# A mixer kernel: the z1 phase in an order fixed at build time, with edits to the first weights, the out operands and the last product

## The chip, the cores and the metric

The kernel runs on one core of one Trainium2 chip. The metric is device microseconds of one execution; lower is better. The five runs before the change took 671.44, 673.53, 670.41, 671.85 and 672.18 us, median 671.85. The engines are named as the profile names them: PE multiplies matrices (PEld is its loading of weights), DVE works on vectors, ACT evaluates functions and copies, POOL is a third engine that is hardly used, and SP (SyncE) only issues DMAs.

## What is computed

Two branches read the same x of 2048 tokens by 1024 features, and a gate mixes them:

```
g   = sigmoid(sum(x * gate_w))                 # per token
qkv = x @ wqkv                                 # 32 heads of 32
a   = softmax(q . k of 8 tokens at distance 0, 2, .., 14) v  @ wo
z   = gelu(x @ w_in)                           # 3584 columns: z1 | z2
z2  = layernorm(z2)
b   = (z1 * (w_sp @ z2 + b_sp)) @ w_out        # w_sp mixes tokens, 2048 x 2048
out = g * a + (1 - g) * b
```

All inputs are bfloat16.

## The kernel before

**Stages.** In the profiled execution PE passes through these, in us from the start of the span: start-up to 15.3 (filler matmuls L313, transposes of x L221, first value tiles L298); query, key and value tiles (L288, L298), with the attention bands (L350) between them; value products from 86.7 to 117.4; further attention work to 195; the z2 half of x @ w_in to 277.4; the z1 half to 361.5; the spatial product w_sp @ z2 from 363 to 532; the output product, which takes w_out and wo together, to 666.6.

**Quads.** From 86.7 us on, matmuls come in "quads": a 2 by 2 block product done with seven products instead of eight, as Strassen and Winograd do. `strassen` (L434) and `chain` (L485) are generators that yield after each product, and `run` interleaves two of them. A product is a row of matmuls (L431) of 128 by 128 by 320, 448 or 512 columns that add up in one bank of PSUM. Four banks make a side, X, Y, Z and V, and two sides alternate. Sums of operand blocks are made ahead by DVE (`sums4`, L563 to L570); sums of results are formed by copying one bank into another (ACT, L449, L460, L470, L504), by DVE adding a saved share (L492; in z1 the share is saved by L1052), and by letting later products add on top. So a PE product waits for the ACT copy or the DVE addition that frees or seeds its bank.

**Start-up.** gw_s (the gate weights) and the first half of the first value weights wvp are issued on ACT's queue; SP issues the first rows of x, the second half of wvp, and more of x in a fixed chain. `keep_warm` (L311) issues filler matmuls into bank 7. The program then transposes x's first rows (`xpose(0)`), and the gate column is transposed and copied by L321 into wvp, which every value tile (`vp_tile`, L293) reads. `vp_tile(i)` puts the next `xpose` in its middle, after two of its eight matmuls. Query and key tiles (`qk_tile`, L284) take banks in turn from `half_bank`; L301 reads the bank of the value tiles.

**Order of the work.** Attention and quads are emitted while a planner is live: it keeps a clock for PE, ACT, DVE, SP and the DMA engines, each operation has a cost and a due time, `advance` (L750) emits what is due, and the order of each engine is pinned to that of emission (`settle`). `due` holds DMAs, `streams` the three attention streams (L690 to L703 are their DVE work), and `fill` single DVE operations that go in when they are ready. `drain` (L772) empties all of these. Before the change the planner is live up to the end of the first z1 block. There `drain` and `settle` are called, `live` is cleared, and everything behind is ordered by the scheduler, with a few dependencies and priorities put in by hand.

**z1.** Seven blocks `fp`, each two interleaved chain quads (token halves c = 0, 1), 14 products of four 512-column matmuls. Block fp needs its 128 columns of both halves of w1 (`load_w1`, two DMAs of 256 KB into one of three slots), their DVE sums (`w1_sums`), and at its end gelu (ACT, L1056) and a store of z1 (`z_d`) from one of two slots, one for each c. Meanwhile the layernorm of z2 is finished: 26 squares on ACT (L851), run in groups of five or six at the start of blocks 0 to 4 by `between`; moments on DVE and POOL, and 16 normalisations (L989), by `normalize` in fours. The raw w_sp is transposed by DMA (`load_raw`, L191, eight of them in this phase), and its four sums (`wsp_sums`, L1028, L1029, L1034, L1035) are 4096 columns each.

**Spatial and out.** Fourteen strassen quads, seven with c = 0 and then seven with c = 1, of 7 products of 8 matmuls. While c = 1 runs, SP loads the out weights in four pieces after quads 0 to 3, `out_sums` (L1185) forms ot3, a first sum and ot2 after quad 3, and `load_act(0)` fetches the first operand of the out phase after quad 5. ot2 and ot3, and slot 0 of those operands, stand in the place of z2h (the normalised z2), whose columns belong to the blocks fp in turn. The out phase is 8 strassen quads, each product 11 matmuls. The last product of the last quad ends in `c21`: ACT copies one half of the bank (L1257), DVE the other (L1258), and each is stored by its own queue.

Of the kernel before, what the change touches and what calls it, by code (L numbers as in the profile page):

```python
# [13 lines left out]
P = 128  # L14
S = 2048
# [43 lines left out]
def kernel(  # L59
# [109 lines left out]
    nc.scalar.dma_start(wvp[:, 0:4, 0:VP], wq_v[:, 0:4, 2 * D:2 * D + VP])  # L169
    first_dma(xn[:, 0:1, :], x_v[:, 0:1, :])  # L170
    first_dma(wvp[:, 4:8, 0:VP], wq_v[:, 4:8, 2 * D:2 * D + VP])
# [106 lines left out]
    half_bank = [0]  # L278
# [14 lines left out]
    def vp_tile(i, bank=None, middle=None):  # L293
        ps = bank() if bank else banks[i % 2]
        for kt in range(KT):
            if kt == KT // 4 and middle is not None:
                middle()
            nc.tensor.matmul(ps[:, 0:VP + 1], xT[:, kt, i * P:(i + 1) * P], wvp[:, kt, :], start=(kt == 0), stop=(kt == KT - 1))  # L298
# [17 lines left out]
    keep_warm(8)  # L316
    xpose(0)
    keep_warm(2)
    gwT = banks[1][:, 0:KT // 2].bitcast(BF)
    nc.tensor.transpose(gwT, gw_s[:], ident[0:KT, 0:KT])  # L320
    nc.vector.tensor_copy(wvp[:, :, VP:VP + 1], gwT.rearrange("p (k o) -> p k o", o=1))  # L321
    for i in range(4):
# [102 lines left out]
    last_w1 = [None]  # L425
# [8 lines left out]
    def strassen(A11, A12, A22, S1, S2, S3, S4, B11, B21, B22, T1, T2, T3, T4, vs, c11, c12, c21, c22, share=nc.scalar.copy, N=512, flip=False, turn=True, side=None):  # L434
# [35 lines left out]
        seed = nc.scalar.copy(V[:, n], Y[:, n])  # L470
# [8 lines left out]
        pe(dur)  # L479
        product(V, pairs(A22, T4), False, N)  # L480
# [291 lines left out]
    def drain():  # L772
        t = clock["PE"]
        while any(s[1] != () for s in streams) or fill or due:
# [46 lines left out]
    w1_slots = [reg(R_OFF + o, 2048).rearrange("p (k f c) -> p k f c", k=KT, f=2) for o in (36864, 30720, 32768)]  # L821

    def load_w1(fp):
        for f in range(2):
            last_w1[0] = sync.dma_start(w1_slots[fp % 3][:, :, f, :], win_v[:, :, HF * f + fp * P:HF * f + (fp + 1) * P])
# [3 lines left out]
    def w1_steps(fp):  # L829
        w, s = w1_slots[fp % 3], ws_slots[fp % 2]  # L830
        return sums4_steps([s[:, q] for q in range(4)], w[:, 0:4, 0], w[:, 4:8, 0], w[:, 0:4, 1], w[:, 4:8, 1])
# [145 lines left out]
    def normalize(n):  # L977
        sl = slice(n, n + 4)
        s1v = s1[:, 4 * n:4 * (n + 4)].rearrange("p (i c) -> p i c", c=4)
        first = nc.vector.tensor_reduce(mean[:, sl], s1v, AX.X, ALU.add)  # L980
        tc.add_manual_dep(first.ins, last_add[0].ins.name, NOSYNC, reason="behind the additions of the quads")
# [5 lines left out]
        for m in range(n, n + 4):  # L987
            ii = z2_row(m)
            nc.vector.tensor_scalar(z2h[:, ii, :], z2[:, ii, :], mean[:, m:m + 1], rstd[:, m:m + 1],  # L989
                                    ALU.subtract, ALU.mult)  # L990
# [25 lines left out]
    def load_raw(c, a):  # L1016
        row = 4 * c + (a % 4) + 8 * (a // 4)
        inst = sync.dma_start_transpose(raw_slots[c][:, :, a, :], wsp_v[row])
        for x in (last_store, last_w1):
# [300 lines left out]
```

## Time and profile before

| | |
|---|---|
| median of five runs | 671.85 us (670.41 to 673.53) |
| the profiled execution | 671.63 us, span 669.9 us |
| PE busy | 659.6 us, 98% |
| DVE / ACT busy | 448.8 / 293.5 us |
| z1 phase on PE | 277.4 to 361.5 us |
| matmuls of L431 | 2436, 498.9 us |

The span runs from the first to the last recorded instruction. Times in a view count from its start. A view of waits names the instruction that waited, and the one that released it. A window gives how long each engine was busy in a stretch of time, so a stretch in which PE is busy for all of its length has nothing to gain from order. Durations are of single instructions; matmuls overlap their neighbours, so the distance between starts, not the mean duration, is what a matmul costs PE.

### The profile page before, as it was taken

What the parts mean: (1) busy time and instruction counts of PE and PEld (TensorE: products, weight loads), DVE (VectorE), ACT (ScalarE), POOL (GpSimd) and SP (SyncE); (2) the same over time, 40 slices, a digit from 0 to 9 for tenths busy, and PEclk for the clock granted to TensorE, in tenths of its full rate; (3) what the DMA queues carried; (4) which work ended last, traced back from release to release, by engine and by line L of the source; (5) the groups of instructions that cost most, each with busy time, mean ns of one, the idle gap of its engine ahead of it and who ended that gap; (6) DMA issues with size and microseconds to landing.
All of it is one profiled execution on the core that took longest, in us unless ns stands there. A gap on an engine that the chain in (4) does not pass through costs nothing.

```text
span 669.9 us, 10729 instructions
## 1 busy us (share of the span) xinstructions
PE 659.6 (98%) x4185; PEld 316.4 (47%) x4185; DVE 448.8 (67%) x663; ACT 293.5 (44%) x620; POOL 6.8 (1%) x15
## 2 busy tenths in 40 slices
PE   8999999998999999999999999999999999999998
PEld 4544467443445555444444444444444444444443
DVE  2520799966999999996679676897766685333301
ACT  3454676555678677887854212121122112222221
POOL 1000000000000000001000000000000000000000
PEclk9999999998999999999999999999999999999999
DMA  9988563698487040449984478567346598943100
GB/s 236 163 215 224 111 152 96 159 240 180 90 219 181 9 141 14 95 123 243 239 212 158 99 167 167 134 184 223 89 136 162 95 198 194 207 107 100 37 32 31
DMA packets 235683, 98.15 MB, mean 147 GB/s; under 512 B 189792, under 2 KB 221936, under 8 KB 235632
## 3 DMA queue, kind: packets, MB, share of 16 engines
q1 hardware_dynamic: 234944, 97.01, 60.6%
q8 instruction: 32, 0.52, 0.3%
q10 hardware_dynamic: 688, 0.46, 0.2%
q14 instruction: 19, 0.16, 0.1%
HBM read 45.10 MB, written 36.61 MB: 122 GB/s over the span
## 4 chain that ended last, share of the span: by engine, by line
PE 94%; DVE 2%; DMA 2%; ACT 1%; issue 0%; SPq 0%; ACTq 0%
PE psum_all L431 72%; PE psum_all L288 16%; PE psum_all L298 3%; PE psum_all L350 1%; DMA band_d<-arena 1%; PE psum_all L313 1%; DVE arena L694 1%; ACT arena L358 1%; DMA arena<-o_d 0%; DVE psum_all L492 0%; PE psum_all L808 0%; ACT arena L300 0%; DVE arena L1136 0%; ACT L801 0%; DVE arena L1131 0%
## 5 line engine op out<-in xcount | busy, mean ns | idle before, releaser
L431 PE MATMUL psum_all<-arena 128*128 128x512 f16 (+5 forms) x2436 | 498.9, 367 | 1.6 <-DVE psum_all L492 1.0
L431 PEld LDWEIGHTS <-arena 128*128 128x128 f16 (+1 forms) x2436 | 238.2, 98 | 261.1 <-issue 4.2
L288 PE MATMUL psum_all<-arena 128*128 128x512 bf16 x512 | 116.1, 383 | 0.7 <-ACT gl_s L301 0.6
L288 PEld LDWEIGHTS <-arena 128*128 128x128 bf16 x512 | 48.8, 98 | 58.1 <-issue 3.0
L694 DVE TENSOR_TENSOR arena<-arena,att_A 128x2048 f16<-128x2048 bf16 (+1 forms) x44 | 73.4, 1704 | 0.3
L291 ACT CAST arena<-psum_all 128x512 bf16<-128x512 f32 x64 | 37.2, 585 | 49.7 <-PE psum_all L288 49.6
L567 DVE TENSOR_TENSOR arena<-arena 128x1024 f16<-128x1024 f16 (+3 forms) x36 | 20.6, 583 | 53.2 <-PE psum_all L431 32.2
L449 ACT COPY psum_all<-psum_all 128x512 f32<-128x512 f32 (+1 forms) x30 | 15.8, 527 | 78.4 <-PE psum_all L431 77.7
L801 ACT ACTIVATE arena<-psum_all 128x448 bf16<-128x448 f32 x64 | 34.2, 544 | 17.6 <-DVE psum_all L492 8.6
L1056 ACT ACTIVATE arena<-psum_all 128x512 bf16<-128x512 f32 x56 | 30.3, 599 | 21.7 <-DVE psum_all L492 10.8
L569 DVE TENSOR_TENSOR arena<-arena 128x1024 f16<-128x1024 f16 (+3 forms) x36 | 20.5, 581 | 28.0 <-PE psum_all L431 13.0
L492 DVE TENSOR_TENSOR psum_all<-psum_all,arena 128x448 f32<-128x448 f32 (+1 forms) x58 | 36.6, 659 | 3.7 <-PE psum_all L431 3.0
L358 ACT CAST arena<-psum_all 128x1988 f16<-128x1988 f32 (+3 forms) x25 | 33.9, 1356 | 7.8 <-DMA band_d<-arena 6.5
L698 DVE TENSOR_TENSOR arena<-arena 128x2048 f16<-128x2048 f16 (+1 forms) x22 | 37.2, 1704 | 0.1
L470 ACT COPY psum_all<-psum_all 128x512 f32<-128x512 f32 (+1 forms) x30 | 15.9, 529 | 46.1 <-PE psum_all L431 45.1
L460 ACT COPY psum_all<-psum_all 128x512 f32<-128x512 f32 (+1 forms) x30 | 15.8, 528 | 40.6 <-PE psum_all L431 40.0
L455 ACT COPY arena<-psum_all 128x512 f32<-128x512 f32 (+1 forms) x30 | 16.2, 543 | 35.4 <-PE psum_all L431 30.4
L851 ACT ACTIVATE arena<-arena 128x896 bf16<-128x896 bf16 x32 | 30.1, 951 | 0.0
L568 DVE TENSOR_TENSOR arena<-arena 128x1024 f16<-128x1024 f16 (+3 forms) x36 | 20.6, 582 | 8.1 <-PE psum_all L431 7.9
L1243 DVE TENSOR_TENSOR arena<-psum_all,arena 128x512 bf16<-128x512 f32 x8 | 5.5, 691 | 29.0 <-ACT psum_all L470 29.0
L298 PE MATMUL psum_all<-arena 128*128 128x385 bf16 x128 | 22.6, 327 | 0.3 <-DVE arena L321 0.3
L570 DVE TENSOR_TENSOR arena<-arena 128x1024 f16<-128x1024 f16 (+3 forms) x36 | 20.4, 579 | 1.7 <-PE psum_all L431 1.6
(88 smaller groups left out, 391.4 us busy)
## 6 DMA issues: line engine op xcount, KB each, us to landing
arena<-v_d SPq DMA_DIRECT2D x8, 960.0 KB, 6.7
z_d<-arena SPq DMA_DIRECT2D x14, 512.0 KB, 4.4
arena<-z_d SPq DMA_DIRECT2D x14, 512.0 KB, 4.3
zg_d<-arena SPq DMA_DIRECT2D x56, 128.0 KB, 2.2
arena<-zg_d SPq DMA_DIRECT2D x32, 224.0 KB, 3.2
band_d<-arena SPq DMA_DIRECT2D x28, 248.5 KB, 5.1
arena<-in_A_wqkv_dram SPq DMA_DIRECT2D x16, 256.0 KB, 4.2
o_d<-arena SPq DMA_DIRECT2D x4, 1024.0 KB, 6.3
```

Of the source, the lines that this page charges most:

```text
L288: nc.tensor.matmul(ps[:], w[:, t, kt, :], xT[:, kt, 512 * c:512 * (c + 1)], start=(kt == 0), stop=(kt == KT - 1))
L291: nc.scalar.copy(dst[:, :, 256 * c:256 * (c + 1)], ps[:].rearrange("p (n e) -> p e n", e=2))
L298: nc.tensor.matmul(ps[:, 0:VP + 1], xT[:, kt, i * P:(i + 1) * P], wvp[:, kt, :], start=(kt == 0), stop=(kt == KT - 1))
L358: nc.scalar.copy(dst, src)
L431: nc.tensor.matmul(bank[:, 0:N], lhsT, rhs, start=(start and m == 0), stop=(m == n - 1), skip_group_check=True)
L492: last_add[0] = nc.vector.tensor_tensor(out[:, n], a[:, n], vs, ALU.add)
L567: first = nc.vector.tensor_tensor(s_out[0], a21, a22, ALU.add)
L694: lambda ws=ws, in0=in0, in1=in1: tt(p5[:, ws], in0[:, ws], in1[:, ws], ALU.mult)), False
L698: lambda a=p3[:, ws], b=p3[:, ws.start + 4:ws.stop + 4]: tt(a, a, b, ALU.add)), not n
L801: nc.scalar.activation(z2[:, i + 8 * a, ZC * c:ZC * (c + 1)], bank[:, 0:ZC], ACT.Gelu_apprx_tanh, accum_out=s1[:, 4 * n + c:4 * n + c + 1])
L851: return nc.scalar.activation(junk, src, ACT.Square, accum_out=(s2, s2h)[x][:, n:n + 1])
L1056: last_gelu[0] = nc.scalar.activation(z1s[:, f, a, :], bank[:], ACT.Gelu_apprx_tanh)
```

## The change

- **First weights.** wvp comes in four pieces of two rows of blocks, the first on ACT's queue, the other three on SP's between x's first two loads. Six filler matmuls, the gate column and two more fillers precede the transposes of x. The first value tile does six of its eight matmuls before the next transposes. The query and key tiles begin one bank further on.
- **z1 phase.** The planner stays live through all seven blocks. After every second product one square is emitted (`z1_step`); moments and normalisations are put into `fill` when their squares are done, one normalisation at a time; the sums of w1 go to the head of `fill`, and the sums of w_sp for c = 0 become eight operations of 2048 columns in blocks 5 and 6. `drain` is called after block 1 and no longer empties `fill`.
- **w1.** Block 0 has its own slot. From there on, each half of w1 is loaded 256 columns wide, for blocks 1 and 2, 3 and 4, 5 and 6, in two DMAs of 512 KB.
- **Other transfers of that phase.** The eight transposes of w_sp are at fixed products of blocks 2 to 4, the z1 store slots are doubled, and the rows bsp and og are loaded after block 4.
- **Out operands.** ot2, ot3 and operand slot 0 move to z2h columns of blocks 0 to 4. ot2 and ot3 become four chunks of 128 columns, apart in memory (`spread`). All out weights are loaded after quads 0 and 1 of c = 1, the sums are made in three parts after quads 2, 3 and 4, and `load_act(0)` comes after quad 4.
- **Last product.** It is computed as two halves of 256 columns in two banks (`cut`), the upper half first. ACT copies the upper half, DVE the lower, and both are stored by SP.

Cut to what matters:

```diff
-    nc.scalar.dma_start(wvp[:, 0:4, 0:VP], wq_v[:, 0:4, 2 * D:2 * D + VP])
+    def load_wvp(k, dma):
+        dma(wvp[:, k:k + 2, 0:VP], wq_v[:, k:k + 2, 2 * D:2 * D + VP])
+    load_wvp(0, nc.scalar.dma_start)
     first_dma(xn[:, 0:1, :], x_v[:, 0:1, :])
-    first_dma(wvp[:, 4:8, 0:VP], wq_v[:, 4:8, 2 * D:2 * D + VP])
+    for k in range(2, KT, 2):
+        load_wvp(k, first_dma)
...
-    half_bank = [0]
+    half_bank = [1]
...
-            if kt == KT // 4 and middle is not None:
+            if kt == (2 if i else 6) and middle is not None:
...
-    keep_warm(8)
-    xpose(0)
-    keep_warm(2)
+    keep_warm(6)
     gwT = banks[1][:, 0:KT // 2].bitcast(BF)
     nc.tensor.transpose(gwT, gw_s[:], ident[0:KT, 0:KT])
     nc.vector.tensor_copy(wvp[:, :, VP:VP + 1], gwT.rearrange("p (k o) -> p k o", o=1))
+    keep_warm(2)
+    xpose(0)
...
+        lo, hi = slice(0, cut or N), slice(cut, N)
+        if cut:
+            nc.scalar.copy(X[:, hi], Y[:, hi])
+        seed = nc.scalar.copy(V[:, lo], Y[:, lo])
...
+            for bank, half in ((X, hi), (V, lo)):
+                ab = pairs(A22, [t[:, half] for t in T4])
+                for m, (lhsT, rhs) in enumerate(ab):
+                    nc.tensor.matmul(bank[:, half], lhsT, rhs, start=False, stop=(m == len(ab) - 1), skip_group_check=True)
+                c21(bank, half)
+            return
...
-        while any(s[1] != () for s in streams) or fill or due:
+        while any(s[1] != () for s in streams) or due:
...
-    w1_slots = [reg(R_OFF + o, 2048).rearrange("p (k f c) -> p k f c", k=KT, f=2) for o in (36864, 30720, 32768)]
+    w1_first = reg(R_OFF + 36864, 2048).rearrange("p (k f c) -> p f k c", k=KT, f=2)
+    w1_pairs = [[reg(R_OFF + o, 2048).rearrange("p (k c) -> p k c", k=KT) for o in at] for at in ((30720, 32768), (24576, 36864))]
+    def w1_half(fp, f):
+        return w1_first[:, f] if fp == 0 else w1_pairs[(fp - 1) // 2 % 2][f][:, :, (fp - 1) % 2 * P:((fp - 1) % 2 + 1) * P]
     def load_w1(fp):
         for f in range(2):
-            last_w1[0] = sync.dma_start(w1_slots[fp % 3][:, :, f, :], win_v[:, :, HF * f + fp * P:HF * f + (fp + 1) * P])
+            to = w1_first[:, f] if fp == 0 else w1_pairs[(fp - 1) // 2 % 2][f]
+            sync.dma_start(to, win_v[:, :, HF * f + fp * P:HF * f + (fp + (2 if fp else 1)) * P])
...
-    def normalize(n):
+    def moments(n):
         sl = slice(n, n + 4)
         s1v = s1[:, 4 * n:4 * (n + 4)].rearrange("p (i c) -> p i c", c=4)
-        first = nc.vector.tensor_reduce(mean[:, sl], s1v, AX.X, ALU.add)
-        tc.add_manual_dep(first.ins, last_add[0].ins.name, NOSYNC, reason="behind the additions of the quads")
+        nc.vector.tensor_tensor(s2[:, sl], s2h[:, sl], s2[:, sl], ALU.add)
+        nc.vector.tensor_reduce(mean[:, sl], s1v, AX.X, ALU.add)
         nc.vector.tensor_scalar(mean[:, sl], mean[:, sl], 1.0 / FH, None, ALU.mult)
         nc.vector.tensor_tensor(var[:, sl], mean[:, sl], mean[:, sl], ALU.mult)
         nc.vector.scalar_tensor_tensor(var[:, sl], s2[:, sl], 1.0 / FH, var[:, sl], ALU.mult, ALU.subtract)
         nc.vector.tensor_scalar(var[:, sl], var[:, sl], 0.0, EPS, ALU.max, ALU.add)
         nc.gpsimd.tensor_tensor(rstd[:, sl], var[:, sl], cm05[:, sl], ALU.pow)
-        for m in range(n, n + 4):
-            ii = z2_row(m)
-            nc.vector.tensor_scalar(z2h[:, ii, :], z2[:, ii, :], mean[:, m:m + 1], rstd[:, m:m + 1],
-                                    ALU.subtract, ALU.mult)
+        fill.extend((clock["DVE"] + 2.5, 0.7, lambda m=m: normalize(m)) for m in range(n, n + 4))
+    def normalize(m):
+        ii = z2_row(m)
+        nc.vector.tensor_scalar(z2h[:, ii, :], z2[:, ii, :], mean[:, m:m + 1], rstd[:, m:m + 1], ALU.subtract, ALU.mult)
...
-        for x in (last_store, last_w1):
-            tc.add_manual_dep(inst.ins, x[0].ins.name, NOSYNC, reason="behind the stores and the loads")
+        if c:
+            tc.add_manual_dep(inst.ins, last_store[0].ins.name, NOSYNC, reason="behind the stores")
...
+        tt = nc.vector.tensor_tensor
+        if c == 0:
+            for n in (0, 4):
+                i, hi = slice(n, n + 4), slice(8 + n, 12 + n)
+                a, b, d, e = raw[:, i, 0:512], raw[:, i, 512:1024], raw[:, hi, 0:512], raw[:, hi, 512:1024]
+                t1, t2, t3 = (t[:, i] for t in t_sum)
+                if part == 0:
+                    yield lambda t1=t1, a=a, b=b: tt(t1, b, a, ALU.subtract)
+                    yield lambda b=b, e=e, h=half[:, i, 512:1024]: tt(h, e, b, ALU.subtract)
+                else:
+                    yield lambda t1=t1, t2=t2, e=e: tt(t2, e, t1, ALU.subtract)
+                    yield lambda t2=t2, t3=t3, d=d: tt(t3, d, t2, ALU.subtract)
...
+    z1s_slots = [[free(o + 2048 * r, 2048).rearrange("p (f a t) -> p f a t", f=2, a=2) for r in range(2)] for o in (T1_OFF, R_OFF + 16384)]
...
+    w1_left = [0]
     def w1_sums(fp):
-        w, s = w1_slots[fp % 3], ws_slots[fp % 2]
-        sums4([s[:, q] for q in range(4)], w[:, 0:4, 0], w[:, 4:8, 0], w[:, 0:4, 1], w[:, 4:8, 1])
+        def one(f):
+            f()
+            w1_left[0] -= 1
+        steps = [(0.0, 0.34, lambda f=f: one(f)) for f in w1_steps(fp)]
+        w1_left[0] += len(steps)
+        fill[:0] = steps
+    def load_rows():
+        sync.dma_start(bsp_bc, bass.AP(tensor=B_b_sp.tensor, offset=B_b_sp.offset, ap=[[0, P], [1, S]]))
+        sync.dma_start(omg_bc, bass.AP(tensor=og_d.tensor, offset=og_d.offset, ap=[[0, P], [1, S]]))
...
-    def between(fp):
-        left = max(5 - fp, 1)
-        for _ in range(-(-len(squares) // left)):
-            act(0.95, clock["PE"])
-            sq = square(*squares.pop(0), z1_junk)
-            tc.add_manual_dep(sq.ins, last_seed[0].ins.name, NOSYNC, reason="behind the first copies of the quads")
+    def z1_step(fp, at):
+        step()
+        at[0] += 1
+        if at[0] % 2 == 0 and squares:
+            act(0.5, clock["PE"])
+            square(*squares.pop(0), z1_junk)
+        n = ready[0]
+        if all(s[1] == () for s in streams) and n + 4 <= (squares[0][0] if squares else 16):
+            fill.append((clock["ACT"] + 0.5, 1.0, lambda n=n: moments(n)))
+            ready[0] += 4
+        if fp == NFH - 1 and at[0] == 2:
+            fill.extend((0.0, 1.15, f) for f in wsp_sums(0, 1))
     mark([b[1] for b in bank_roles], 512, ZC)
-    for fp in (1, 2):
-        dma(clock["PE"] + 1.0, 2.9, lambda fp=fp: load_w1(fp), w1_landed(1) if fp == 1 else None)
+    dma(clock["PE"] + 1.0, 2.9, lambda: load_w1(1), w1_landed(1))
+    RAW_AT = {2: {2: 0, 4: 1, 6: 2}, 3: {4: 3, 6: 4}, 4: {2: 5, 4: 6, 6: 7}}
     for fp in range(NFH):
+        while w1_left[0]:
+            advance(max(clock["PE"], clock["DVE"]) + 0.5)
         if 0 < fp < NFH - 1:
             w1_sums(fp + 1)
-        raws = ((), (0,), (1, 2), (3, 4), (5, 6), (7,), ())[fp]
-        for a in raws[:1]:
-            load_raw(0, a)
-        if fp == 6:
-            wsp_sums(0, 0)
+        if fp == NFH - 2:
+            fill.extend((clock["PE"] + 3.0, 1.15, f) for f in wsp_sums(0, 0))
         late = () if fp else [b[2] for b in bank_roles]
-        run(z1_quad(fp, 0), z1_quad(fp, 1), hooks={2: lambda: between(fp), 3: lambda: mark(late, 512, ZC), 4: lambda: [load_raw(0, a) for a in raws[1:]]},
-            step=None if fp else step)
-        if fp == 0:
+        at = [0]
+        run(z1_quad(fp, 0), z1_quad(fp, 1), hooks={3: lambda: mark(late, 512, ZC), **{n: lambda a=a: load_raw(0, a) for n, a in RAW_AT.get(fp, {}).items()}},
+            step=lambda: z1_step(fp, at))
+        if fp == 1:
             drain()
-            settle()
-            live[0] = False
-            pinned.clear()
-        while fp and ready[0] + 4 <= (squares[0][0] if squares else 16):
-            n = ready[0]
-            nc.vector.tensor_tensor(s2[:, n:n + 4], s2h[:, n:n + 4], s2[:, n:n + 4], ALU.add)
-            with tc.high_priority() if n == 12 else nullcontext():
-                normalize(n)
-            ready[0] += 4
-        if fp + 3 < NFH:
+        if fp in (0, 2):
             load_w1(fp + 3)
+        if fp == NFH - 3:
+            load_rows()
+    while fill:
+        advance(max(clock["PE"], clock["DVE"]) + 0.5)
+    settle()
+    live[0] = False
+    pinned.clear()
...
-    ot3, ot2 = z2h[:, 0:KOH, 0:512], z2h[:, 0:KOH, HF:HF + 512]
+    def spread(off):
+        return [z2h[:, 4 * (k % 4):4 * (k % 4) + 4, off + P * (k // 4):off + P * (k // 4 + 1)] for k in range(KOH)]
+    ot3, ot2 = spread(2 * P), spread(HF + 2 * P)
+    def spread_rows(off, k0, k1):
+        return z2h[:, 0:4 * (k1 - k0), off + P * (k0 // 4):off + P * (k0 // 4 + 1)].rearrange("p (k x) c -> p k x c", x=4)
...
-    SPL = ((0, 5), (5, KOH))
-    def out_sums():
-        for k0, k1 in SPL:
-            nc.vector.tensor_tensor(ot3[:, k0:k1], wrows(KOH + k0, KOH + k1, 1), wrows(k0, k1, 1), ALU.subtract)
-            nc.vector.tensor_tensor(wrows(k0, k1, 1, True), wrows(k0, k1, 1), wrows(k0, k1, 0), ALU.subtract)
-            nc.vector.tensor_tensor(ot2[:, k0:k1], wrows(KOH + k0, KOH + k1, 1), wrows(k0, k1, 1, True), ALU.subtract)
+    SPL = ((0, 4), (4, 8), (8, KOH))
+    def chunks(w):
+        return w.rearrange("p k (x c) -> p k x c", c=P)
+    def out_sums(n):
+        k0, k1 = SPL[n]
+        w11, w12, w22 = (chunks(w) for w in (wrows(k0, k1, 0), wrows(k0, k1, 1), wrows(KOH + k0, KOH + k1, 1)))
+        t1 = chunks(wrows(k0, k1, 1, True))
+        nc.vector.tensor_tensor(spread_rows(2 * P, k0, k1), w22, w12, ALU.subtract)
+        nc.vector.tensor_tensor(t1, w12, w11, ALU.subtract)
+        nc.vector.tensor_tensor(spread_rows(HF + 2 * P, k0, k1), w22, t1, ALU.subtract)
     def out_sums_late():
         for k0, k1 in SPL:
-            nc.vector.tensor_tensor(ot4[:, k0:k1], wrows(KOH + k0, KOH + k1, 0), ot2[:, k0:k1], ALU.subtract)
+            nc.vector.tensor_tensor(chunks(ot4[:, k0:k1]), chunks(wrows(KOH + k0, KOH + k1, 0)), spread_rows(HF + 2 * P, k0, k1), ALU.subtract)
...
-                d[dt] = [z[:, 0:KOH, 512 + HF * x:512 + HF * x + 256].rearrange("p k (a t) -> p k a t", a=2) for x in range(2)]
+                d[dt] = [z[:, 0:KOH, HF * x:HF * x + 256].rearrange("p k (a t) -> p k a t", a=2) for x in range(2)]
...
-            nc.scalar.copy(ob[:, 1, 0:256], V[:, 0:256])
-            nc.vector.tensor_copy(ob[:, 1, 256:512], V[:, 256:512])
-            for x, q in ((0, nc.scalar.dma_start), (1, sync.dma_start)):
-                q(out2[(i + 8) * P:(i + 9) * P, 256 * x:256 * x + 256], ob[:, 1, 256 * x:256 * x + 256])
+            if half.start:
+                nc.scalar.copy(ob[:, 1, half], V[:, half])
+            else:
+                nc.vector.tensor_copy(ob[:, 1, half], V[:, half])
+            sync.dma_start(out2[(i + 8) * P:(i + 9) * P, half], ob[:, 1, half])
...
+                 [wrow(k, 1, True) for k in KH], ot2, ot3,
+                 [ot4[:, k, :] for k in KH], vs, c11, c12, c21, c22, cut=256 * (i == 7)))
...
-    sync.dma_start(bsp_bc, bass.AP(tensor=B_b_sp.tensor, offset=B_b_sp.offset, ap=[[0, P], [1, S]]))
-    sync.dma_start(omg_bc, bass.AP(tensor=og_d.tensor, offset=og_d.offset, ap=[[0, P], [1, S]]))
-    wsp_sums(0, 1)
...
-        if fp < 4:
+        if fp < 2:
             load_out_weights(fp)
-        if fp == 3:
-            out_sums()
-        if fp == 5:
+            load_out_weights(fp + 2)
+        if fp in (2, 3, 4):
+            out_sums(fp - 2)
+        if fp == 4:
```

## The prediction

> **What bounds the kernel now.** I read the head of the page first, then PE's waits, then the windows, then the timeline where a window is not full.
>
> ```profile
> span 669.9 us, 10729 instructions
> ...
> PE 659.6 (98%) x4185; PEld 316.4 (47%) x4185; DVE 448.8 (67%) x663; ACT 293.5 (44%) x620; POOL 6.8 (1%) x15
> ...
> PE 94%; DVE 2%; DMA 2%; ACT 1%; issue 0%; SPq 0%; ACTq 0%
> ```
>
> TensorE (PE) is busy 98% of the span and holds 94% of the chain that ended last. No matmul is removed, so the change can only fill the 10.3 us (669.9 − 659.6) in which PE is idle, or shorten matmuls that run slowly.
>
> ```profile
> 540.00:660.00 120.00, 120.00 (x557) 54.39 (x556) 41.87 (x76) 25.36 (x44) 0.00 (x0) 1.00 0.51 115
> ```
>
> Columns: stretch, its length, busy time (count) of PE, weight loads, DVE, ACT, POOL, then granted clock, DMA share, GB/s. Here 557 matmuls of 512 columns fill 120 us: 0.2155 us each, which no reordering improves. So I looked for the excess of each matmul's start-to-start time over 0.2155 us. The large ones show among PE's waits (line, releaser: total, times, longest):
>
> ```profile
> PE psum_all L350 <- ACT arena L358: 2.6, 2, 2.2
> PE psum_all L313 <- DVE arena L308: 1.2, 1, 1.2
> PE psum_all L431 <- DVE psum_all L492: 1.0, 2, 0.8
> PE psum_all L288 <- ACT gl_s L301: 0.6, 1, 0.6
> PE psum_all L431 <- DVE arena L1136: 0.4, 1, 0.4
> PE psum_all L298 <- DVE arena L321: 0.3, 1, 0.3
> ```
>
> The first (attention bands near 161 and 192 us, behind band stores) and the second (first instruction) are not touched. The others are.
>
> **Start-up.** The timeline gives start, length, engine, line, shape and count:
>
> ```profile
> 5.74 1.01 PE L313 MATMUL psum_all<-arena 128*128 128x512 bf16 x2
> ...
> 7.14 0.49 PE L298 MATMUL psum_all<-arena 128*128 128x385 bf16 x2 [0.28 <-DVE arena L321]
> ...
> 15.32 1.02 PE L288 MATMUL psum_all<-arena 128*128 128x512 bf16 x4 [0.63 <-ACT gl_s L301]
> ```
>
> Two filler matmuls and a wait for the gate column (L321) stand between the first transposes and the first value tile, whose eight matmuls end at about 9.1. Afterwards the fillers and the gate column go first. The eight transposes then run at about 4.9 to 5.7. Six matmuls of the tile follow once the weights are there, at about 6.1. At 1.47 / 8 = 0.184 us each (the later row "L298 x8") they take 1.1 us, the next transposes 0.45 (0.68 with their waits), the last two 0.37: the tile ends at 8.0, 1.1 us sooner. The wait of 0.63 at 15.32 goes too, since the first query/key tile gets another bank than the one L301 reads. Sum 1.73 us.
>
> The weight pieces must land by then. Before, the two halves land at 5.20 (SyncE's queue) and 6.11 (ACT's). Now 196 KB are on ACT's queue and three times 196 KB on SP's, the same bytes in all, ahead of x1, which landed at 6.55. x1, x2, x3 (256 KB each) land at 6.55, 7.22, 7.92, 0.65 to 0.70 us apart, so pieces of one queue overlap and I charge the two extra issues 0.1 us.
>
> The Trainium skill ("DMA: Bandwidth & Descriptors", Anatomy of one DMA, and Measured) speaks against pieces: each DMA has a fixed cost of about 2.0 us, mostly the confirmation of its last byte, and it wants 1 MiB a piece. Were these costs paid one after another, two more pieces would cost 4 us and the start-up would be about 2.3 us slower instead of 1.7 faster; the landings 0.65 us apart say they are not.
>
> How much of 1.73 lasts? From 9 to 50 us the transfers limit ACT and DVE: L300 waits 2.9 us for a value store near 31, L358 1.4 near 44, and DVE's attention work starts at 64.2 on a DMA; none of that moves with PE. DVE is then the late engine, but idles 0.48 + 0.66 + 0.44 + 0.59 = 2.2 us before L613 between 92 and 117, enough to take 1.7 up. If it can't, 0.3 lasts. I take 1.4, nearer to the idle rows.
>
> **z1 phase (277.4 to 361.5 us).** Seven blocks of 56 matmuls, 12.07 us each. PE loses 0.96 near 308, 0.14 near 337, 0.27 near 361: 1.37 us, in the first of these windows mostly.
>
> ```profile
> 301.60:313.70 12.10, 11.30 (x54) 5.05 (x52) 9.52 (x17) 8.07 (x18) 2.50 (x2) 1.00 1.03 260
> 313.70:325.70 12.00, 12.00 (x57) 5.42 (x56) 6.16 (x14) 10.01 (x21) 0.00 (x0) 1.00 1.07 238
> ```
>
> At 308 L492, which frees a bank, stands behind six normalisations (L989, 0.74 us each) in DVE's order, and ACT's gelus behind five or six squares in bulk. The new order places squares singly, after every second product, normalisations singly, and cuts the four w_sp sums of 4096 columns (2.28 us) into eight of 2048 (1.22 us by L694): +0.64 us of DVE work where DVE was busy 9.2 and 11.6 us of a block. That fits: I find 0.6 to 1.9 us of slack at each insertion.
>
> ACT is tighter. Five squares and their reads run from 317.01 to 321.68, 0.93 each; six gelus take 3.15, 0.525 each; two copies 1.13. Seven squares, eight gelus, two copies make 6.5 + 4.2 + 1.1 = 11.8 us of 12.07, in three blocks. Bounds: nothing lost, or up to 0.5 us in each of these three if a copy that PE needs stands behind one square. I take 0.25, nearer to nothing as gelus here have a whole product to wait: 1.37 − 0.25 = 1.1.
>
> DMAs that this order waits on: w1 for two blocks now comes as two issues of 512 KB. A 512 KB store takes 4.7 us to land here, a 256 KB w_in load 4.7 too, so the first pair (second half issued about 1.4 us before the phase) lands 3 to 5 us into it and is needed at about 7. DVE stood 6.8 us waiting for w_in before at no price to PE; a late load now would hold the shares queued behind it. The og and bsp rows move from 277 and 337 to after block 4; their users start in the spatial phase. The eight transposes of w_sp are the slow rival below.
>
> **Second half of the spatial phase, and out.** Excesses: 0.20 at 501, 0.53 at 531, 0.15 at 534, 0.125 at 540, sum 1.0, where the out weights, their sums (L1184 to L1189), the last spatial sums (L1136) and the first out sums come together:
>
> ```profile
> 523.80:531.40 7.60, 7.29 (x34) 3.23 (x33) 6.16 (x12) 0.57 (x1) 0.00 (x0) 1.00 0.51 66
> 531.40:540.00 8.60, 8.55 (x39) 3.81 (x39) 8.60 (x13) 1.74 (x3) 0.00 (x0) 1.00 0.93 211
> ```
>
> DVE is full where PE misses. With weights loaded after blocks 0 and 1 and sums in thirds after 2, 3 and 4, this work lies where DVE had room (113.7 of 158.8 us busy from 365 to 523.8). Cutting adds about 0.16 us an operation (2 × 1.22 − 2.28), covered there. I take 0.85 of 1.0.
>
> New here: the moving operands ot2 and ot3 become four chunks of 128 columns with a stride, for 2 × 11 × 8 = 176 matmuls. No row has such an operand. Below: nothing, since as many columns stream. Above: if each chunk cost what a separate 128-column matmul does (eight L221 in 0.68 us, 0.085 each against 0.054 for a quarter of 0.2155), 4 × 0.031 × 176 = 22 us. I take nothing: no weights or issues come with a chunk, and mean durations of 299, 353 and 379 ns for 320, 448 and 512 columns follow the columns alone.
>
> **End.** PE ends at 666.57, ACT copies half of the last bank (0.37), and DVE the other half only after it:
>
> ```profile
> 666.59 0.37 ACT L1257 CAST arena<-psum_all 128x256 bf16<-128x256 f32 x1 [4.12 <-PE psum_all L431]
> ...
> 666.99 0.42 DVE L1258 CAST arena<-psum_all 128x256 bf16<-128x256 f32 x1 [2.08 <-ACT arena L1257]
> ```
>
> With the product computed in halves in two banks, ACT's half is copied under the second half, and DVE starts at PE's end: −0.40. The cost is 11 more matmuls and weight loads; 22 loads of 0.098 us fit beside 2.37 us of matmuls, so 0.05. Gain 0.35.
>
> **Sum.** 1.4 + 1.1 + 0.85 + 0.35 = 3.7 us. The profiled execution took 671.63 us, 0.2 below the median of 671.85: 671.63 − 3.7 = **667.9 us**.
>
> **Rivals.** (1) All of it lasts: 1.73 + 1.37 + 1.0 + 0.4 = 4.5, 667.1. (2) Gains given back: the start-up keeps 0.3 because transfers and not PE pace attention, ACT's full blocks eat two times 0.5 of z1 (0.3 left), out keeps 0.75, the end 0.25: 1.6, 670.0. For it: DVE is busy 57.7 of 60 us from 200 to 260 (the windows), so a late DVE would not recover there; against it: its 2.2 us of idle before. (3) The w_sp transposes come late: slower. SyncE starts them once the o store has landed, some 29 us into the phase, as before; a transpose held SyncE 3.36 us in the mean (26.9 / 8; up to 5.6) and landed up to 8.5 us after issue. At the mean the last lands by about 29 + 7 × 3.36 + 8.5 = 61 (63.5 with the stores between); the first w_sp sum stands in DVE's fixed order at about 66.2. At 5.3 us each it lands at 74.6, 8.4 late, all shares behind it wait, and the time is 667.9 + 8.4 = 676. It decides from about 4.9 us each, where the lateness exceeds the gain by 2 us. DMA share was 1.03 to 1.07 while they ran and the doubled w1 loads fall there too; against it, total bytes don't grow. (4) The stride costs PE: from 8 ns a chunk (5.7 / 704) the change is slower; at a tenth of the bound above, 670; at half, 679.
>
> **Chances.** Forecast 0.50, rival 1 0.15, 2 0.22, 3 0.09, 4 0.04. A measurement of this kernel tells about 0.3% (2.0 us) from no change, so faster 0.65, same 0.22, slower 0.13. The range reaches from 666.4 (rival 1 less 0.1% of spread) to 671.9 (rival 2 with the lost ACT block doubled): 0.87 of the cases, less their tails.
>
> **What the profile would show.** L288 first at 13.6 to 13.9 us without a wait on L301, and the distance kept to L431's first (86.7 before); no PE wait on L492 between 275 and 360, with L1056 no longer held up to 2.3 us; PE full from 520 to 540; DVE's last copy starting with PE's end. Wrong would be: a new wait of DVE on w_sp or w_in transfers with PE waits behind it, ACT copies (L504) late in z1 blocks 0 to 2, or products with ot2 longer than 11 × 0.2155.

## The result, and the profile after

The changed kernel took 669.73 us (median of 35 runs, 667.88 to 672.02) against 671.98 us (59 runs) before: ratio 0.9968, interval 0.9961 to 0.9976, or 2.2 us less. That is faster, inside the range, and 1.8 us short of the 667.9 that was forecast. Run again beside its variants the ratio was 0.9949 (0.9930 to 0.9969).

The profiled execution took 668.07 us, 3.6 less than the profiled one of before, as if the forecast had been exact. It was not: the two differ by luck as well. These are the windows from 163 to 167 us, before and after:

```profile
163.00:167.00 4.00, 3.13 (x62) 1.48 (x62) 2.42 (x5) 3.61 (x4) 0.00 (x0) 0.59 0.68 108
```
```profile
163.00:167.00 4.00, 3.88 (x72) 2.06 (x72) 2.62 (x6) 3.15 (x5) 0.00 (x0) 1.00 0.67 114
```

The clock column reads 0.59 before: behind its longest wait (2.2 us, near 161) PE ran some matmuls at 0.43 us a start, 1.36 us lost. After it reads 1.00 behind a wait of 2.3 us. Of the 35 runs of the changed kernel 13 had a mean clock of 0.997 and a median of 670.66, those with 1.0 had 669.43: the half clock comes and goes from execution to execution. Without it, the profiles differ by 3.6 − 1.36 = 2.2 us, what the medians say; but that they agree so well is luck too, since the profiled run after is itself 1.4 us below the 669.43 of its kind.

PE's waits after:

```profile
PE psum_all L354 <- ACT arena L362: 2.7, 2, 2.3
PE psum_all L317 <- DVE arena L312: 1.2, 1, 1.2
PE psum_all L292 <- ACT gl_s L305: 0.9, 1, 0.9
PE psum_all L434 <- DVE psum_all L505: 0.8, 2, 0.6
PE psum_all L225 <- DMA arena<-in_A_x_dram: 0.6, 1, 0.6
```

The wait on L305 looks like the old one on L301, but it stands at 32.8 instead of 15.3 us. The waits on the spatial sums and on the gate column are gone. From the last loss of the z2 phase on, PE lost nothing over 0.1 us. The windows of one z1 block and of the end of the spatial phase, PE busy for the whole of each:

```profile
299.90:312.00 12.10, 12.10 (x57) 5.47 (x56) 9.86 (x26) 11.76 (x25) 2.46 (x2) 1.00 0.69 205
522.00:538.00 16.00, 16.00 (x75) 7.24 (x74) 10.83 (x16) 2.87 (x5) 0.00 (x0) 1.00 0.91 189
```

ACT is 11.76 of 12.10 us busy, as full as was worked out, and it held nothing up. At the start, the timeline:

```profile
6.96 0.85 PE L225 MATMUL psum_all<-ident,arena 128*128 128x128 bf16 x8 [0.57 <-DMA arena<-in_A_x_dram]
...
13.38 0.81 PE L292 MATMUL psum_all<-arena 128*128 128x512 bf16 x3
```

The first query/key tile comes at 13.38 instead of 15.32, 1.94 us sooner. Where do they go? ACT's copy of the values (L300, now L304) waits for the store that frees its slot, and the store does not land sooner. ACT's timeline near 32 us, before and after, and PE's after:

```profile
31.43 0.48 ACT L300 CAST arena<-psum_all 128x384 bf16<-128x384 f32 x1 [2.88 <-DMA v_d<-arena]
```
```profile
32.18 0.48 ACT L304 CAST arena<-psum_all 128x384 bf16<-128x384 f32 x1 [5.57 <-DMA v_d<-arena]
```
```profile
32.77 3.60 PE L292 MATMUL psum_all<-arena 128*128 128x512 bf16 x15 [0.94 <-ACT gl_s L305]
```

ACT waited 2.88 us before, while PE still had other work. Now it waits 5.57 us, and PE stands behind it. The chain of work that ended last after the change, in order of time (start, length, what):

```profile
0.74 0.40 SPq L162
...
23.12 1.31 SPq L179
...
28.68 3.40 DMA v_d<-arena
32.72 1.48 ACT arena L362
34.20 0.38 ACT arena L304
34.70 3.61 PE psum_all L292 x16
...
154.29 8.46 DMA band_d<-arena
162.82 2.48 DMA att_L<-band_d
...
196.54 2.29 DVE arena L707
...
200.95 0.64 DVE psum_all L505
201.62 65.32 PE psum_all L434 x344
```

Before, this chain ran on PE from 1.19 to 152 us. Now it starts on SyncE, which issues transfers one behind another up to 28.7 us, and passes through the store of values to ACT's copies. From 34.7 to 147.7 us it is on PE, and then it runs through band transfers and DVE's attention products to 201 us. In the first and the last of these stretches PE is no longer the late one. The end:

```profile
661.79 0.37 ACT L1311 CAST arena<-psum_all 128x256 bf16<-128x256 f32 x1 [2.89 <-PE psum_all L490]
662.99 0.42 DVE L1313 CAST arena<-psum_all 128x256 bf16<-128x256 f32 x1 [1.71 <-PE psum_all L490]
```

ACT copies its half 1.2 us sooner than DVE, which waits for PE alone.

### The profile page after: what moved, and what is told of

It reads as the page before. It is cut to its first block, busy times and chain, and to the rows that moved or that the text cites. A ratio compares the mean times of both kernels' runs of the same rounds, so it can differ in the third digit from the quotient of the medians.

```text
span 666.2 us, 10753 instructions
## 1 busy us (share of the span) xinstructions
PE 656.1 (98%) x4194; PEld 316.1 (47%) x4194; DVE 451.5 (68%) x671; ACT 292.4 (44%) x621; POOL 6.6 (1%) x15
## 4 chain that ended last, share of the span: by engine, by line
PE 85%; DVE 6%; SPq 4%; DMA 3%; issue 1%; ACT 0%; ACTq 0%; DVEq 0%
PE psum_all L434 72%; PE psum_all L292 11%; SPq L179 3%; DVE arena L707 3%; DMA band_d<-arena 1%; SPq L162 1%; DVE arena L711 1%; PE psum_all L354 1%; DMA att_L<-band_d 1%; PE psum_all L302 1%; DVE arena L712 1%; DMA v_d<-arena 1%; PE psum_all L490 0%; DVE arena L716 0%; SPq L190 0%
## 5 line engine op out<-in xcount | busy, mean ns | idle before, releaser
L434 PE MATMUL psum_all<-arena 128*128 128x512 bf16 (+5 forms) x2425 | 495.8, 367 | 0.9 <-DVE psum_all L505 0.8
L707 DVE TENSOR_TENSOR arena<-arena,att_A 128x2048 f16<-128x2048 bf16 (+1 forms) x44 | 73.5, 1706 | 0.3
L580 DVE TENSOR_TENSOR arena<-arena 128x1024 f16<-128x1024 f16 (+3 forms) x31 | 18.9, 610 | 48.5 <-PE psum_all L434 41.7
L452 ACT COPY psum_all<-psum_all 128x512 f32<-128x512 f32 (+1 forms) x30 | 15.8, 527 | 76.8 <-PE psum_all L434 73.0
L1094 ACT ACTIVATE arena<-psum_all 128x512 bf16<-128x512 f32 x56 | 31.2, 602 | 21.5 <-PE psum_all L434 13.1
L505 DVE TENSOR_TENSOR psum_all<-psum_all,arena 128x448 f32<-128x448 f32 (+1 forms) x58 | 37.0, 661 | 4.1 <-PE psum_all L434 3.4
L582 DVE TENSOR_TENSOR arena<-arena 128x1024 f16<-128x1024 f16 (+3 forms) x31 | 18.7, 609 | 30.9 <-PE psum_all L434 18.0
L711 DVE TENSOR_TENSOR arena<-arena 128x2048 f16<-128x2048 f16 (+1 forms) x22 | 37.2, 1705 | 0.1
L476 ACT COPY psum_all<-psum_all 128x512 f32<-128x512 f32 (+2 forms) x30 | 15.6, 522 | 46.2 <-PE psum_all L434 45.2
L463 ACT COPY psum_all<-psum_all 128x512 f32<-128x512 f32 (+1 forms) x30 | 15.8, 528 | 36.4 <-PE psum_all L434 35.6
L581 DVE TENSOR_TENSOR arena<-arena 128x1024 f16<-128x1024 f16 (+3 forms) x31 | 18.5, 610 | 10.4 <-PE psum_all L434 10.3
L576 DVE TENSOR_TENSOR arena<-arena 128x512 f16<-128x512 bf16 (+3 forms) x36 | 19.4, 569 | 3.6 <-DMA arena<-in_B_w_in_dram 2.1
```

The lines of the kernel that those rows point to most:

```text
L434: nc.tensor.matmul(bank[:, 0:N], lhsT, rhs, start=(start and m == 0), stop=(m == n - 1), skip_group_check=True)
L505: last_add[0] = nc.vector.tensor_tensor(out[:, n], a[:, n], vs, ALU.add)
L707: lambda ws=ws, in0=in0, in1=in1: tt(p5[:, ws], in0[:, ws], in1[:, ws], ALU.mult)), False
L711: lambda a=p3[:, ws], b=p3[:, ws.start + 4:ws.stop + 4]: tt(a, a, b, ALU.add)), not n
L1094: last_gelu[0] = nc.scalar.activation(z1s[:, f, a, :], bank[:], ACT.Gelu_apprx_tanh)
```

## The experiments

Theory: the start-up's gain is given back, because up to 200 us the transfers and DVE, not PE, set the pace; what counts is z1, the out operands and the end. Rival: the forecast's sum, with 1.4 us of the start-up lasting. Two numbers from the starts of matmuls are used below. "z2 mark" is the start of the second of the three losses that every profile shows at the end of z2 (mostly 0.25, 0.39 and 0.16 us); "rest" is the time from there to PE's end, taken as 0.2155 us behind the start of the last matmul of 512 columns, or half of that for 256. Losses in us.

| kernel | ratio (interval) | 31 to 46 | near 161 | near 200 | z2 mark | rest |
|---|---|---|---|---|---|---|
| before | | | 2.4, half clock 1.36 | | 274.2 | 392.2 |
| changed | 0.9968 (0.9961–0.9976) | 1.1 | 2.5 | 0.76 | 272.9 | 389.9 |
| e1 start-up only | 1.0003 (0.9991–1.0015) | 1.36 | 1.4 | 0.76 | 272.0 | 392.5 |
| e2 old start-up | 0.9970 (0.9957–0.9984) | | 0.8 | 0.52 | 272.3 | 389.9 |
| e3 z1 only | 0.9981 (0.9968–0.9994) | | 2.5 | 0.38 | 272.8 | 391.5 |
| e4 out only | 0.9976 (0.9962–0.9990) | | 1.1 | 0.89 | 271.6 | 391.1 |
| e5 changed again | 0.9949 (0.9930–0.9969) | 1.6 | 2.0 | 0.39 | 272.6 | 389.9 |
| e6 third slot | 0.9943 (0.9925–0.9961) | 1.3 | 1.3 | 0.55 | 271.4 | 389.9 |
| e7 tile ahead | 1.0017 (1.0005–1.0030) | 1.6 | 0.0 | 4.1, half clock 1.6 | 276.0 | 389.7 |
| e8 fillers | 0.9955 (0.9937–0.9972) | 0.5 | filled | 0 | 271.1 | 389.9 |
| e9 w1 single | 0.9940 (0.9916–0.9964) | 1.3 | 2.3, half clock 1.7 | 0 | 273.5 | 389.9 |
| e10 norms in fours | 0.9955 (0.9938–0.9973) | 0.8 | 1.5 | 1.21 | 272.1 | 390.5 |
| e11 squares in bulk | 0.9949 (0.9932–0.9966) | 1.6 | 0.0 | 0.95 | 271.3 | 389.9 |
| e12 fine, slot | 0.9957 (0.9940–0.9974) | 2.3 | 1.5 | 0.95 | 273.0 | 390.6 |

e1 to e4 shared their runs of before, e5 to e8 theirs, e9 to e12 theirs, these on another chip; kernels of one group compare best.

Where the start-up's lead goes can be read from the starts of the query/key matmuls in all fourteen profiles. The first one starts at 14.6 to 15.8 us in the four with the old start-up and at 13.2 to 13.7 in the ten with the new one, 1.8 us apart in the mean. The 41st starts at 34.6 to 35.8 us and, in the eight of the ten that have two value slots, at 34.2 to 35.4, 0.3 us apart. So nearly all of the lead is gone by 36 us. From 49 to 139 us no profile loses more than 0.2 us before one matmul; what comes near 161 and 200 differs by more than this rest from execution to execution.

**e1: the start-up edits alone.** The first four parts of the diff in the kernel before (weight pieces, `half_bank`, the middle of `vp_tile`, the order of fillers and gate column).

> The kernel before with the start-up edits alone (four weight pieces, order of fillers, gate column and first tile, first bank). Theory 'given back': PE reaches its first query/key tile 1.9 us sooner (13.4 instead of 15.3), then loses 1.3 us near 31 to 34 us to the copy that waits for a value store, and more near 200 us, so at the z2 quads little is left: 0 to 0.6 us faster than before, ratio 0.999 to 1.000. Rival, as forecast: 1.4 us lasts, ratio 0.9979.

No gain that can be told: 1.0003, and the rival's 0.9979 lies outside the interval. PE's waits of this kernel:

```profile
PE psum_all L354 <- ACT arena L362: 1.4, 3, 0.7
...
PE psum_all L292 <- ACT gl_s L305: 1.2, 1, 1.2
```

The second line is the new wait near 32 us: the store that frees the value slot lands no sooner (ACT's copy behind it starts at 32.5 us, before at 31.4). It stands in SyncE's order behind x's transposes, which SyncE issues one after another up to 24.7 us (24.8 before). No run shortens these transposes, so what the lead would be worth without them is not shown.

**e2: the change with the old start-up.** The same four parts undone.

> The changed kernel with the start-up of before. Theory 'given back': the z1 phase, the out operands and the end make up 2.4 us by themselves, so 1.7 to 2.4 us faster than before, ratio 0.9965 to 0.9975, like the whole change (0.9968). Rival, that 1.4 us of the start-up last and the other parts are worth only 0.9: ratio 0.9987.

0.9970, as good as the whole change. Its z2 mark lies at 272.3, between those of e1 and the changed kernel with the new start-up (272.0 and 272.9). Over the profiles without half clock the mark varies from 271.1 to 273.0, and it does not follow the start-up.

**e3: the z1 phase alone.** The parts from `drain` to the loop over `fp`, without out operands and `cut`.

> The kernel before with the z1 phase of the change alone (fixed order, w1 loads for two blocks, doubled store slots, split spatial-weight sums). Theory: PE's losses of 0.96, 0.14 and 0.27 us in that phase go and nothing new comes: 1.4 us faster, ratio 0.998, no excess over 0.1 us between 280 and 362 us. Rival: the out operands need it and it gives less than 0.5, or the late w_sp transposes show as a new wait: ratio 0.9993 or more.

0.9981, and the z1 losses are gone. The rest is 391.5; without the losses of 1.60 us that e3 still has between 498 and 538 it is 389.9.

**e4: the out operands alone.** `spread`, three parts of the sums, weights and operand slot 0, without `cut`.

> The kernel before with the edit of the out operands alone (ot2, ot3 and operand slot 0 in other z2h columns, in chunks; weights, sums and first operands earlier), without the last product in halves. Theory: the losses at 501, 531, 534 and 540 us go, 1.0 us in all: ratio 0.9985, and products with the chunked operands take 11 x 0.2155 us as before. Rival, strided chunks cost PE: those products are longer and the ratio is 0.9995 or more.

0.9976, somewhat more than expected, with the expected 0.9985 in its interval. The losses from 501 to 540 are gone, and the chunked products are not longer. In the windows of e4 and, for contrast, of e1, whose end of the spatial phase is the old one:

```profile
522.00:538.00 16.00, 16.00 (x76) 7.26 (x75) 11.14 (x17) 2.87 (x5) 0.00 (x0) 1.00 0.97 198
```
```profile
522.00:538.00 16.00, 15.14 (x71) 6.74 (x69) 14.62 (x22) 2.31 (x4) 0.00 (x0) 1.00 0.63 148
```

With the old operands DVE is 14.62 of 16 us busy and PE misses 0.86; spread out, DVE has 11.14 and PE misses nothing. Which part of the edit does it (the other place, the earlier loads, the sums in three parts) was not separated. In e1 and e3 the four losses sum to 1.49 and 1.60 us, not to the 1.0 of the first profile: what the edit is worth differs by execution.

**e5, e6: the change again, and with a third value slot.** e6:

```diff
-    vp_slots = [... for o in (36288, 37824)]
+    vp_slots = [... for o in (36288, 37824, 4096)]
...
-        st = vp_slots[(i // 4) % 2]
+        st = vp_slots[(i // 4) % 3]
```

> The changed kernel once more, beside its variants. Both theories: ratio 0.9968 to before, within 0.001. In its profile the theory 'given back' expects PE to lose about 1.3 us near 31 to 34, and between 0.7 and 2.5 near 161 and 0.3 to 0.9 near 200, the two in exchange for one another.

> The changed kernel with a third slot for the first value tiles, so that their copy near 32 us no longer waits for a store. Theory 'DVE and the band transfers set the pace up to 200 us': the loss of 1.3 us near 31 to 34 goes, PE comes sooner to 161 and 200 us and waits that much longer there; ratio as for the changed kernel (0.9968), within 0.0007. Rival, that the gain of the start-up was lost at this copy: 1.1 to 1.3 us faster than the changed kernel, ratio 0.995.

e5's 0.9949 missed the expected 0.9968 by 0.0019, the same kernel against other runs of before; its waits came about as expected. e6 is level with e5 (667.25 against 667.63), but six runs of each are too few to exclude the rival's 1.1 us. The profile says more: the loss at 31 went, as meant, and came back at 46 and not, as expected, near 161. There the gate's matmul waits for the same line of ACT, and ACT for a band store, 3.9 us where it was 1.4 before. PE's wait and ACT's:

```profile
PE psum_all L404 <- ACT gl_s L305: 1.1, 1, 1.1
```
```profile
ACT arena L362 <- DMA band_d<-arena: 3.9, 1, 3.9
```

So the copy near 32 is not the only place where the gain is lost; it is the first one behind the transfers.

**e7: a tile ahead of the wait near 161.**

```diff
+        if g == 5:
+            return [tiles[0], band[0], tiles[1], band[1], tiles[2], tiles[3], tiles[4], band[2]] + tiles[5:]
```

> The changed kernel with one query/key tile (1.73 us of PE) moved ahead of the band matmuls that wait near 161 us. Theory 'DVE and the band transfers set the pace up to 200 us': the wait at 161 falls from 0.85 to 2.4 us to below 0.7, the loss at 200 us grows instead; at most 0.4 us faster than the changed kernel, ratio 0.9962 to 0.9972. Rival, that PE's time before 200 us counts: 0.85 to 1.7 us faster than the changed kernel, ratio 0.9943 to 0.9955.

Neither: it was 4.3 us slower than e5. The wait at 161 vanished and 4.1 us came at 200, with half clock behind it. DVE's timeline:

```profile
194.18 2.29 DVE L707 TENSOR_TENSOR arena<-arena,att_A 128x4096 f16<-128x4096 bf16 x1
...
197.53 2.28 DVE L707 TENSOR_TENSOR arena<-arena,att_A 128x4096 f16<-128x4096 bf16 x1
...
200.06 2.29 DVE L711 TENSOR_TENSOR arena<-arena 128x4096 f16<-128x4096 f16 x1
202.26 1.16 DVE L505 TENSOR_TENSOR psum_all<-psum_all,arena 128x448 f32<-128x448 f32 x2
```

PE needs L505, and the planner, whose clocks the moved tile had shifted, put it behind one more operation of 4096 columns (L711; in e5 it follows the two of L707). So e7 moves two things and settles nothing on size; that the wait reappears where DVE is late agrees with the theory.

**e8: fillers in that wait.**

```diff
+            if g == 5 and x == 2:
+                for _ in range(8):
+                    nc.tensor.matmul(banks[(half_bank[0] + 1) % 4], xT[:, 4, 0:P], xT[:, 4, 0:512], ...)
```

> The changed kernel with eight filler matmuls of 512 columns (1.72 us) ahead of the same band matmuls, into a free bank, so that PE is busy in its longest wait. Theory 'the pace is set elsewhere': no change beside the changed kernel within 0.4 us, even where the wait is shorter than the fillers, and no matmuls at half clock after the wait. Rival, that the half clock after this wait costs whole executions 1.3 us: median 0.4 to 0.5 us better and no granted clock of 0.997. Rival, that the fillers delay the path: 0.3 to 0.9 us slower.

667.75, level with e5: 1.7 us of additional PE work in this wait cost nothing that the runs can tell. Single runs spread from 666.2 to 669.5 us, so the last rival's 0.3 to 0.9 us is not excluded by them; the profile shows no loss near 200 and the earliest z2 mark of all, 271.1. No clock below 0.999 was seen in its eight runs, but e5's six had none either, so what the fillers do for the clock stays open.

**e9, e10, e11: parts of the z1 edit undone.** e9 loads w1 for one block at a time; e10 puts four normalisations right behind their moments, in one piece; e11 emits the squares in bulk at each block's start. The edits of e9, e10 and e11:

```diff
-            sync.dma_start(to, win_v[:, :, HF * f + fp * P:HF * f + (fp + (2 if fp else 1)) * P])
+            for n in range(2 if fp else 1):
+                sync.dma_start(w1_half(fp + n, f), win_v[:, :, HF * f + (fp + n) * P:HF * f + (fp + n + 1) * P])
...
-        fill.extend((clock["DVE"] + 2.5, 0.7, lambda m=m: normalize(m)) for m in range(n, n + 4))
+        for m in range(n, n + 4):
+            normalize(m)
...
-            fill.append((clock["ACT"] + 0.5, 1.0, lambda n=n: moments(n)))
+            fill.append((clock["ACT"] + 0.5, 4.9, lambda n=n: moments(n)))
...
-        if at[0] % 2 == 0 and squares:
-            act(0.5, clock["PE"])
-            square(*squares.pop(0), z1_junk)
+        if at[0] == 2:
+            for _ in range(min(len(squares), (6, 5, 5, 5, 5, 0, 0)[fp])):
+                act(0.95, clock["PE"])
+                square(*squares.pop(0), z1_junk)
```

> The changed kernel with w1 loaded 128 columns at a time again (four DMAs of 256 KB for a pair of blocks instead of two of 512 KB), everything else as changed. Theory 'these transfers are hidden': from 275 us to PE's end as in the changed kernel (389.9 us from the loss near 274 us on), no PE wait in z1; ratio 0.995 to 0.997. Rival, that the double loads are what keeps w1 in time in the fixed order: a new PE wait of 0.3 to 2 us in the first z1 blocks.

> The changed kernel with four normalisations at once right behind their moments, as one piece of DVE's order, POOL's step included (before: the same shape). Theory 'the z1 losses came from additions queued behind normalisations': PE loses 0.3 to 1.0 us in some of blocks 1 to 4 again, 390.3 to 392 us from the loss near 274 us to PE's end. Rival, that the bulk of ACT's squares caused them: 389.9 us as in the changed kernel.

> The changed kernel with the squares in groups of six and five at the start of blocks 0 to 4, as before, normalisations still single. Theory 'the z1 losses came from additions queued behind normalisations': 389.9 us from the loss near 274 us to PE's end, or at most 0.4 more. Rival, that the squares in bulk held ACT's copies and gelus: 0.5 to 1.4 us more.

The rest is 389.9 in e9 and e11 and 390.5 in e10, whose single loss (0.58) stands at 369 in the spatial phase and not in z1; so its 390.5 lies in the range that the theory named, but not for the theory's reason. Neither the width of the loads nor the size of the groups, each undone alone, makes z1's gain. What is left is the order that the planner fixes, and parts that no run took out: the doubled store slots, the halved sums of w_sp and the places of its transposes. The traces speak for the order. DVE's timeline before, where PE lost 0.96 us:

```profile
302.78 4.03 DVE L989 TENSOR_SCALAR arena<-arena,mean,rstd 128x1792 f16<-128x1792 bf16 x6 [1.14 <-POOL rstd L986]
306.72 1.28 DVE L1052 COPY arena<-psum_all 128x512 f32<-128x512 f32 x2
307.92 0.74 DVE L989 TENSOR_SCALAR arena<-arena,mean,rstd 128x1792 f16<-128x1792 bf16 x1
308.57 1.29 DVE L492 TENSOR_TENSOR psum_all<-psum_all,arena 128x512 f32<-128x512 f32 x2
```

Six normalisations, then the shares, one more, and only then the additions that PE waits for. In the changed kernel:

```profile
307.15 0.74 DVE L1009 TENSOR_SCALAR arena<-arena,mean,rstd 128x1792 f16<-128x1792 bf16 x1
308.14 0.70 DVE L505 TENSOR_TENSOR psum_all<-psum_all,arena 128x512 f32<-128x512 f32 x1 [0.24 <-PE psum_all L434]
309.00 0.70 DVE L505 TENSOR_TENSOR psum_all<-psum_all,arena 128x512 f32<-128x512 f32 x1 [0.16 <-PE psum_all L434]
```

One normalisation goes ahead, and DVE then waits for PE before each addition, not PE for DVE. Here and in e10 the planner has a length for what it inserts (0.7 us for a normalisation, 4.9 for e10's piece), and in both a row of four follows such additions. A kernel with single operations in a wrong order was not tried, so that the order makes the gain is argued from these lines and not shown by a run of its own.

**e12: a candidate.** The third slot, and DVE's 4096-column products of group 4 cut in two (`FINE` 3 instead of 4).

> A candidate: the changed kernel with the third value slot, and DVE's two products of 4096 columns near 197 us (4.49 us ahead of an addition that PE needs) cut to four of 2048. Theory: the loss near 200 us (0.4 to 0.9) falls by half or goes, while the losses near 272 to 276 us, set by DVE as well, grow by no more than half of that; PE reaches its mark near 274 us 0.3 to 1 us sooner than the changed kernel, ratio 0.993 to 0.996. Rival, that DVE is the bound over the whole of 65 to 275 us: the loss moves into 272 to 276 us, the cuts add 0.16 us each, ratio 0.997 or more.

668.37, no better than e9 to e11 in the same group. The loss near 200 stayed at 0.95, and another of 0.57 came at 331 in z1. No version clearly beat the changed kernel; e6 and e2 are level with it.

## Why the prediction was right or wrong

- **Start-up, size.** Right: 1.73 us forecast, 1.94 measured in the first pair of profiles and 1.8 in the mean of all; the first tile ends near 8.0, the bank wait is gone. The weight pieces cost little: they landed 0.5 to 0.8 us apart, x's second block came at 6.91 instead of 6.55, and PE waited 0.57 for it. The 2.0 us that the forecast quotes from the Trainium skill ("DMA: Bandwidth & Descriptors", Anatomy of one DMA) stand there for DMAs issued from GpSimd; these were issued by SyncE and ACT.
- **Start-up, what lasts.** This step failed: "I take 1.4" was about nothing (e1 1.0003; e2 0.9970 beside 0.9968). I had named the limit myself, as rival 2 (transfers pace attention, L300 waits 2.9 us for a value store), then argued that DVE's 2.2 us of idle between 92 and 117 us would absorb it. The lead never got there. Moved-up PE work does not move the store that ACT waits for: ACT's wait grew from 2.9 to 5.6 us, and as PE was now early enough to need ACT's bank, 0.5 to 1.6 us became PE's own wait near 32 us in the eight profiles with the new start-up and two value slots, a step that I had not followed. The sign that I named for a lead that lasts failed with it: the distance to L431's first matmul was not kept (85.9 us against 86.5 before, 0.6 sooner and not 1.9). DVE is not what took the lead: its first product of 4096 columns follows the 161st query/key matmul by 2.77 to 2.78 us in all fourteen profiles. The 0.3 us that I named for the case that it does not last, without saying from what, is near the 0.3 us that the mean of the starts still shows at 35 us.
- **z1.** 1.1 forecast, 1.1 to 1.4 measured (the z1 losses sum to 1.4 us before and to 1.1 and 1.2 in e1 and e4, which have the old z1). ACT at 97% cost nothing, so the 0.25 held back for it was too cautious. The mechanism was half right: going by e10 and e11 it is not the single pieces, and going by the timelines it is the order. One sign did not come and cost nothing: L1056 (now L1094) is still held by DVE's additions, up to 2.6 us. The w1 pairs are neutral (e9).
- **Transposes of w_sp and strided chunks, rivals 3 and 4.** Neither came: no z1 wait on w_sp in the changed kernel, and the rest is the same 389.9 with the losses subtracted, chunks or not.
- **Out.** 0.85 forecast; the losses it removes are 1.0 in the first profile and 1.5 to 1.6 in e1 and e3.
- **End.** 0.35 forecast. From PE's end to the span's end it took 3.5 to 3.8 us in four profiles with the old end and 3.2 to 3.4 in ten with the new one, about 0.25 less; the additional matmuls cost 0.05 (389.92 against 389.87), as worked out. No run has this edit alone.
- **Sum.** 0 + 1.3 + 1.0 to 1.5 + 0.2 = 2.5 to 3.0 us, against 2.2 and 3.6 in the two comparisons of the changed kernel. What stays open is why these two differ; their intervals overlap. So the total came near the forecast with one term of 1.4 us at about nothing, made good in part by the others. The upper end of the range does not come out of its own terms: rival 2 with the two lost 0.5 us doubled is 671.0, not 671.9. The result lies below both.

## What to carry to other kernels

A gain at the start of a pipeline lasts only if whatever else is late moves too: before counting it, follow each transfer and each second engine to the next point where PE waits for them, or would wait if it came sooner, and ask what sets their times. Losses behind the last such point add up almost exactly. And look at the clock in the windows of both profiles before believing a difference of one execution.

## What was not expected of the hardware

- A wait of PE of 2.2 us near 161 was followed by a clock of 0.59 in one window of 4 us, and waits of about the same length in other profiles (2.3 us in the changed kernel) were not. The Trainium skill ("TensorE: Matmul & The Clock Gate", What's actually happening) puts the return to half clock at an idle window of about 3.4 us that runs freely. The granted clock in the trace stood at 0.50 for 3.41 us in one piece (163.73 to 167.14 us; as long in e7 and e9), which fits the length of that window, and a free-running phase fits runs that differ. That PE must be idle for 3.4 us does not fit, as 2.2 us of waiting was enough here.
- The same spatial phase lost 0.53 us before one matmul in the first profile and 1.02 and 1.13 in e1 and e3, with the same instructions.
